# Seven quarter products in place of eight: one level of Strassen's algorithm in the second FFN product

## The chip, the cores and the metric

The kernel runs on one core of one Trainium2 chip. The metric is the device time of one execution in microseconds (us), as a median over runs. The span that the profile shows is 1.5 to 2 us shorter than that time, so I compare spans with spans and times with times. Ratios are the mean time of one kernel's fast runs over that of the other's fast runs of the same rounds, so they are not quite the ratios of the medians quoted beside them. Each comes with a 95% interval.

## The reference, cut to what matters

Eight batches. In each, 512 rows of x and 32 rows of a state attend to each other, in 8 heads of 64 columns; the result goes through an FFN with an exact GELU.

```python
scores = scale * x @ state^T;   a  = softmax(scores);   xread = a  @ state   # 512 rows a batch
scores2 = scale * state @ x^T;  a2 = softmax(scores2);  sread = a2 @ x       #  32 rows a batch
X = concat([xread, sread])                   # (8 x 544) rows of 512
h = X @ w_in                                 # 512 -> 2048
g = 0.5 * h * (1 + erf(h / sqrt(2)))
out = g @ w_out                              # 2048 -> 512: the "second FFN product"
```

For the 512 rows the kernel folds the state into the first weight (P = state @ w_in, per head), so the first product is only `a^T @ P`. The second product is the largest piece of work: for each batch a 512 x 2048 by 2048 x 512 matrix product.

## The kernel before

All operands are bf16, all sums are kept in f32 in PSUM. One batch goes through eight steps; in each step TensorE makes two blocks of 128 columns of h (`M`) and two quarters of an output tile (`U`), so that ScalarE's GELUs of one block run beside the matmuls of another. `[...]` marks cuts.

```python
def mm1(b, m):                               # first product, block m of 16
    [...]
    hp = ps_f.tile([128, S], FP32, name="hp", tag="f")
    for t in range(2):
        nc.tensor.matmul(hp, lhsT=Ps[b][:, t, m * 128:(m + 1) * 128],
                         rhs=atts[b].AT[:, :, t, :], start=(t == 0), stop=(t == 1))
    nc.scalar.activation(out=gs[b][:, m, :], in_=hp, func=AF.Gelu)

def mm2(b, q, j):                            # second product: 4 of the 16 blocks, rows j of 4
    [...]
    for m in range(4 * q, 4 * q + 4):
        nc.tensor.matmul(ps, lhsT=gs[b][:, m, j * 128:(j + 1) * 128],
                         rhs=w_out_bf[:, m, :], start=(m == 0), stop=(m == MC - 1))
    if q == 3:
        [...]
        evac(ps, [...])                      # VectorE copies PSUM to SBUF, SyncE issues the output

u = 17
for b in range(1, B):
    nb = b + 1
    for p in range(2 if b == 1 else 0, 8):
        k = 16 * b + 2 * p
        if p == (4 if b == 1 else 1) and nb < B:
            scores(nb, 0); scores(nb, 1)     # reads xT of the next batch
            [...]
        if b > 1 and p in (3, 4) and nb < B:
            norm(nb, p - 3)
        if p == (7 if b == 1 else 5) and nb < B:
            atr_dma(nb)                      # DMA transpose of the attention matrix: AT
        if p == 5 and nb + 1 < B:
            begin(nb + 1)
            rearr(nb + 1)                    # GpSimd copies of x
            xtr_dma(nb + 1)                  # DMA transpose of x: xT, two batches ahead
            rearr_ones(nb + 1)               # GpSimd copies of x
        M(k, k + 1)
        [...]
        while u < k - 4:
            U(u)
            u += 1
        if p == 2 and b > 1:
            burst([(b, 2), (b, 3)] + ([(nb, 0), (nb, 1)] if nb < B else []), b)   # P chunks
        if p == 6 and b + 3 < B:
            [...]
            load_x(b + 3)                    # GpSimd issues the load of x, three batches ahead
```

Both transposes and all outputs are issued by SyncE, into one DMA queue; the loads of x are issued by GpSimd into another.

The softmax here doesn't subtract the row's maximum and nothing guards it: scores larger than these inputs give would overflow.

Of the kernel before, what the change touches and what calls it, by code (L numbers as in the profile page):

```python
# [17 lines left out]
def kernel(  # L18
# [8 lines left out]
    nc = tc.nc  # L27
# [11 lines left out]
    persist = ctx.enter_context(tc.tile_pool(name="persist", bufs=1))  # L39
    xin = ctx.enter_context(tc.tile_pool(name="xin", bufs=3))  # L40
    att = ctx.enter_context(tc.tile_pool(name="att", bufs=2))
    gpool = ctx.enter_context(tc.tile_pool(name="gpool", bufs=3))
    opool = ctx.enter_context(tc.tile_pool(name="opool", bufs=4))
    PSUM = bass.MemoryType.PSUM
    ps_f = ctx.enter_context(tc.tile_pool(name="ps_f", bufs=4, space=PSUM))
    ps_o = ctx.enter_context(tc.tile_pool(name="ps_o", bufs=4, space=PSUM))

    ctx.enter_context(tc.manual_schedule())



# [5 lines left out]
    g_sr = persist.tile([128, MC, B * NS], BF16, name="g_sr")  # L57
    st_f = persist.tile([128, 2, D], FP32, name="st_f")
    st_bf = persist.tile([128, B, 2, D], BF16, name="st_bf")
    x0f = persist.tile([128, 4, 2, SJ * D], FP32, name="x0f")  # L60
    x0b = persist.tile([128, 4, SJ, 2, D], BF16, name="x0b")
    xT0 = persist.tile([128, 4, SJ, 128], BF16, name="xT0")
    sb0 = persist.tile([128, 2, 2, 2, NS], BF16, name="sb0")
    gate = persist.tile([128, HC], FP32, name="gate")
    hold = persist.tile([128, 1], BF16, name="hold")
# [61 lines left out]


    def keep_warm(n):
        ps = ps_o.tile([128, 512], FP32, name="warm_ps", tag="op")  # L130
        for _ in range(n):
            nc.tensor.matmul(ps[:, 0:128], lhsT=warm, rhs=warm, start=True, stop=True)

# [129 lines left out]

    def scores0(q):
        A = atts[0]
        pc = ps_o.tile([128, SJ, 2 * NS], FP32, name="pc", tag="op")
        for j in range(SJ):
            nc.tensor.matmul(  # L268
                pc[:, j, :],
                lhsT=xT0[:, q, j, :],  # L270
                rhs=sb0[:, q // 2, q % 2, :, :].rearrange("p u n -> p (u n)"),
                start=True,
                stop=True,
            )
        nc.scalar.activation(out=part0(A.e, q), in_=pc, func=AF.Exp, scale=scale)
# [76 lines left out]

    def sread(b):
        A = atts[b]
        pool, tag = (ps_o, "op") if b == B - 1 else (ps_f, "f")
        A.sr = pool.tile([128, 2, 65], FP32, name="sr", tag=tag)
        for t in range(2):
            for j in range(SJ):
                for c in range(HC):
                    nc.tensor.matmul(  # L360
                        A.sr[32 * c:32 * c + 32, t, :],
                        lhsT=A.e[:, 2 * j + t, 32 * c:32 * c + 32],
                        rhs=A.xo[:, j, c, 1 + 65 * t:66 + 65 * t],
                        start=(j == 0),
                        stop=(j == SJ - 1),
                    )
# [21 lines left out]

    Ps = {}

    def p_mm(b, f, pool, tag):
        if b not in Ps:
            Ps[b] = att.tile([128, 2, d_ff], BF16, name="P", tag="P")
        ps = [pool.tile([128, 512], FP32, name="p_ps", tag=tag) for t in range(2)]
        for c in range(HC):
            for t in range(2):
                nc.tensor.matmul(  # L397
# [11 lines left out]
        nc.vector.tensor_copy(out=dst[:, 1, :], in_=ps[1])  # L409

    def pmat(b, f):
        p_copy(b, f, p_mm(b, f, ps_f, "f"))



# [1 line left out]
    def burst(chunks, b_read=None):  # L417
# [2 lines left out]
        if first:  # L420
            sread(b_read)
        for i, (b, f) in enumerate(chunks):
            pool, tag = (ps_f, "f") if i < 2 else (ps_o, "op")
            done.append((b, f, p_mm(b, f, pool, tag)))
        for x in done[:2]:
            p_copy(*x)
        if b_read is not None and not first:
# [9 lines left out]
    def pmat00(h):  # L437
        if h == 0:
            Ps[0] = att.tile([128, 2, d_ff], BF16, name="P", tag="P")
        ps = [ps_o.tile([128, 256], FP32, name="p_ps", tag="op") for t in range(2)]  # L440
        for c in range(HC):
            for t in range(2):
                nc.tensor.matmul(
# [35 lines left out]
        return out[b * SB:b * SB + S, :].rearrange("(p j) n -> j p n", j=SJ)[j]  # L479


    def mm2_last(b, j):
        osb = opool.tile([128, d_model], FP32, name="osb", tag="osb")
        rows = out_rows(b, j)
        for n0, n1, pool, tag in ((0, 384, ps_o, "op"), (384, d_model, ps_f, "f")):
            ps = pool.tile([128, n1 - n0], FP32, name="opl", tag=tag)
            for m in range(MC):
                nc.tensor.matmul(  # L488
                    ps,
                    lhsT=gs[b][:, m, j * 128:(j + 1) * 128],  # L490
                    rhs=w_out_bf[:, m, n0:n1],
                    start=(m == 0),
                    stop=(m == MC - 1),
                )
            if n0 == 0:
                nc.vector.tensor_copy(out=osb[:, n0:n1], in_=ps)
                nc.sync.dma_start(out=rows[:, n0:n1], in_=osb[:, n0:n1])
            else:
                nc.scalar.copy(out=osb[:, n0:n1], in_=ps)  # L499
                nc.scalar.dma_start(out=rows[:, n0:n1], in_=osb[:, n0:n1])  # L500


    def mm2(b, q, j):
        if b == B - 1 and j == SJ - 1:
            return
        if q == 0:
            ops[b, j] = ps_o.tile([128, d_model], FP32, name="op", tag="op")
        ps = ops[b, j]
        for m in range(4 * q, 4 * q + 4):
            nc.tensor.matmul(  # L510
# [11 lines left out]
    def mm1_sr(m):  # L522
# [8 lines left out]
            )  # L531
        nc.scalar.activation(out=g_sr[:, m, :], in_=hp, func=AF.Gelu)

    def mm2_sr(s):
        ps = ps_f.tile([128, d_model], FP32, name="ops", tag="f")
        for m in range(MC):
# [14 lines left out]
    def mm2_m(b, m):  # L551
        for j in range(SJ):
            if m == 0:
                ops[b, j] = ps_o.tile([128, d_model], FP32, name="op", tag="op")
            nc.tensor.matmul(  # L555
                ops[b, j],
                lhsT=gs[b][:, m, j * 128:(j + 1) * 128],
                rhs=w_out_bf[:, m, :],
                start=(m == 0),
                stop=(m == MC - 1),  # L560
            )


    def M(*ms):
# [111 lines left out]


    u = 17
    for b in range(1, B):
        nb = b + 1  # L680
        for p in range(2 if b == 1 else 0, 8):
            k = 16 * b + 2 * p
            if p == (4 if b == 1 else 1) and nb < B:
                scores(nb, 0)
                scores(nb, 1)
                if b == 1:
                    norm(nb, 0)
                    norm(nb, 1)
            if b > 1 and p in (3, 4) and nb < B:
                norm(nb, p - 3)  # L690
            if p == (7 if b == 1 else 5) and nb < B:
                atr_dma(nb)
            if p == 5 and nb + 1 < B:
                begin(nb + 1)
                rearr(nb + 1)
                xtr_dma(nb + 1)
                rearr_ones(nb + 1)
            M(k, k + 1)
            if nb == B and p >= 4:
                for m in range(4 * p - 16, 4 * p - 12):  # L700
                    mm1_sr(m)
            while u < k - 4:
                U(u)
                u += 1
            if p == 2 and b > 1:
                burst([(b, 2), (b, 3)] + ([(nb, 0), (nb, 1)] if nb < B else []), b)
            if p == 6 and b + 3 < B:


                nc.gpsimd.tensor_copy(out=hold, in_=gs[b][:, 12, 0:1])  # L710
                load_x(b + 3)
            if p == 3 and b > 1:
                srt(b)
    while u < 16 * B - 4:
        U(u)
        u += 1
    mm2_sr(0)
    mm2_sr(1)
    U(*range(16 * B - 4, 16 * B - 1))
    mm2_last(B - 1, SJ - 1)  # L720


# [28 lines left out]
```

## Time and profile before

| | before |
|---|---|
| time, us | 216.77 median of 3 (216.36 to 216.99) |
| span in the profile, us | 215.3 |
| TensorE busy | 97% |
| VectorE, ScalarE, GpSimd busy | 38%, 57%, 21% |
| one steady batch in the chain, us | 22.90, without a gap |
| its second product, us | 8 x 1.73 = 13.84 |

The profile lists for each engine the time in which it was busy. The prediction below shows its lines and reads them.

### The profile page before, as it was taken

The page shows a single profiled execution, that of the slowest core. Times are in us where ns is not written, and L with a number is a line of the kernel's source. Part 1 is how long each engine was busy: PE and PEld are TensorE (multiplying, and loading weights), DVE is VectorE, ACT ScalarE, POOL GpSimd, SP SyncE. Part 2 cuts the span into 40 slices and gives each one's busy share as a digit, 9 for nine tenths or more (in the row PEclk, how much of TensorE's full clock was granted, in tenths as well). Part 3 has the DMA queues.
Part 4 walks back from the last instruction along what each step waited for, and adds up shares of the span by engine and source line. Part 5 has one row for each costly group of instructions (what it writes and reads, how often), then busy time and mean ns, then how long its engine had stood idle before and what let it go on. Part 6 is the DMA issues. An engine that isn't in the chain of part 4 may idle for free.

```text
span 215.3 us, 4019 instructions
## 1 busy us (share of the span) xinstructions
PE 208.1 (97%) x1667; PEld 102.4 (48%) x1667; DVE 80.8 (38%) x169; ACT 122.9 (57%) x220; POOL 45.7 (21%) x59
## 2 busy tenths in 40 slices
PE   7699999999999999999999999999999999999994
PEld 6445344444444445444544444444444444766443
DVE  2934474724039202850177005900392025000151
ACT  3954765687686447844874477645864444764000
POOL 8954303911023013301221130300000000000000
PEclk9999999999999999999999999999999999999999
DMA  6999999782822591428450873270225013000034
GB/s 205 173 172 204 205 193 176 182 212 52 97 97 100 97 140 44 160 45 140 63 194 3 156 88 131 67 144 4 100 97 53 0 49 148 3 0 0 6 104 185
DMA packets 40131, 23.11 MB, mean 107 GB/s; under 512 B 22064, under 2 KB 36656, under 8 KB 40112
## 3 DMA queue, kind: packets, MB, share of 16 engines
q0 software_dynamic: 13936, 8.10, 28.0%
q1 hardware_dynamic: 25488, 14.36, 25.1%
q10 hardware_dynamic: 688, 0.39, 0.6%
q8 instruction: 13, 0.21, 0.4%
q14 instruction: 6, 0.05, 0.1%
HBM read 17.30 MB, written 8.91 MB: 122 GB/s over the span
## 4 chain that ended last, share of the span: by engine, by line
PE 89%; DMA 7%; ACT 1%; POOL 0%; issue 0%; SPq 0%; DVE 0%
PE op L510 47%; PE hp L461 24%; DMA w_out_bf<-in_moe_w_out_dram 6%; PE p_ps L397 4%; PE hps L525 3%; PE ops L537 3%; DMA x0f<-in_x_dram 2%; PE op L555 2%; PE opl L488 2%; PE pt L305 1%; PE sr L360 1%; PE xT_ps L233 1%; POOL a L292 0%; PE pc L268 0%; ACT P L451 0%; ACT x0b L219 0%
## 5 line engine op out<-in xcount | busy, mean ns | idle before, releaser
L510 PE MATMUL op<-w_out_bf,g 128*128 128x512 bf16 x464 | 110.1, 379 | 0.4 <-DMA w_out_bf<-in_moe_w_out_dram 0.4
L468 ACT ACTIVATE g<-hp 128x512 bf16<-128x512 f32 x124 | 66.6, 600 | 53.4 <-PE hp L461 53.3
L510 PEld LDWEIGHTS <-g 128*128 128x128 bf16 x464 | 45.2, 98 | 54.5 <-issue 1.6
L461 PE MATMUL hp<-AT,P 128*128 128x512 bf16 x248 | 63.5, 379 | 0.5 <-ACT P L408 0.5
L474 DVE COPY osb<-op 128x512 f32<-128x512 f32 x31 | 21.4, 691 | 85.1 <-PE op L510 85.0
L461 PEld LDWEIGHTS <-P 128*128 128x128 bf16 x248 | 22.9, 98 | 25.8 <-issue 1.0
L408 ACT CAST P<-p_ps 128x512 bf16<-128x512 f32 x31 | 16.3, 595 | 13.6 <-PE p_ps L397 13.6
L409 DVE CAST P<-p_ps 128x512 bf16<-128x512 f32 x31 | 19.9, 682 | 7.5 <-PE p_ps L397 7.4
L201 POOL COPY x<-xb 128x1024 bf16<-128x1024 bf16 x12 | 12.2, 1045 | 33.5 <-DMA xb<-in_x_dram 28.2
L211 POOL COPY xo<-xb 128x1024 bf16<-128x1024 bf16 x12 | 12.2, 1051 | 20.1 <-PE sr L360 20.1
L325 DVE TENSOR_REDUCE cs<-e 128x16 f32<-128x512 bf16 x14 | 9.5, 676 | 4.0 <-ACT e L312 4.0
L397 PE MATMUL p_ps<-w_in_bf,sbd 64*32 64x512 bf16 x248 | 10.3, 381 | 0.0
L312 ACT ACT_TABLE_LOAD x7 | 9.0, 1283 | 1.8 <-issue 1.3
L328 DVE TENSOR_TENSOR a<-e,ics 128x512 bf16<-128x512 bf16 x14 | 9.7, 692 | 0.5
L474 DVE COPY osb<-ops 128x512 f32<-128x512 f32 x2 | 1.4, 692 | 22.5 <-PE ops L537 22.5
L468 ACT ACT_TABLE_LOAD x7 | 9.0, 1283 | 0.1
L499 ACT COPY osb<-opl 128x128 f32<-128x128 f32 x1 | 0.3, 266 | 15.2 <-PE opl L488 15.2
L555 PE MATMUL op<-w_out_bf,g 128*128 128x512 bf16 x32 | 7.7, 380 | 0.0
L312 ACT ACTIVATE e<-pt 128x512 bf16<-128x512 f32 x14 | 7.6, 594 | 0.1
L525 PE MATMUL hps<-XSR,w_in_bf 128*128 128x256 bf16 x64 | 7.6, 272 | 0.0
L710 POOL COPY hold<-g 128x1 bf16<-128x1 bf16 x4 | 0.8, 192 | 29.7 <-ACT g L468 29.7
L537 PE MATMUL ops<-w_out_bf,g_sr 128*128 128x512 bf16 x32 | 7.1, 379 | 0.0
(76 smaller groups left out, 123.2 us busy)
## 6 DMA issues: line engine op xcount, KB each, us to landing
out_dram<-osb SPq DMA_DIRECT2D x25, 256.0 KB, 2.4
xb<-in_x_dram POOLq DMA_DIRECT2D x7, 512.0 KB, 7.3
w_out_bf<-in_moe_w_out_dram POOLq DMA_DIRECT2D x4, 512.0 KB, 13.0
w_in_bf<-in_moe_w_in_dram POOLq DMA_DIRECT2D x6, 256.0 KB, 12.4
out_dram<-osb SPq DMA_DIRECT2D x12, 128.0 KB, 2.0
x0f<-in_x_dram SPq DMA_DIRECT2D x3, 256.0 KB, 3.8
w_in_bf<-in_moe_w_in_dram POOLq DMA_DIRECT2D x4, 128.0 KB, 4.1
out_dram<-osb SPq DMA_DIRECT2D x8, 64.0 KB, 1.7
```

The lines of the kernel that those rows point to most:

```text
L201: nc.gpsimd.tensor_copy(out=A.x4[:, :, :, 64 * t:64 * t + 64].rearrange("p j c d -> p c j d"), in_=src[:, t],)
L211: eng.tensor_copy(out=A.xo[:, :, :, 2 + 64 * t:66 + 64 * t].rearrange("p j c d -> p c j d"), in_=src[:, t],)
L312: nc.scalar.activation(out=A.e[:, :, 64 * half:64 * half + 64], in_=pt.rearrange("p j t c n -> p (j t) (c n)"), func=AF.Exp, scale=scale,)
L397: nc.tensor.matmul(ps[t][32 * c:32 * c + 32, :], lhsT=sbd[64 * t:64 * t + 64, b, c, 32 * t:32 * t + 32], rhs=w_in_bf[64 * t:64 * t + 64, c ...
L408: nc.scalar.copy(out=dst[:, 0, :], in_=ps[0])
L409: nc.vector.tensor_copy(out=dst[:, 1, :], in_=ps[1])
L461: nc.tensor.matmul(hp, lhsT=Ps[b][:, t, m * 128:(m + 1) * 128], rhs=atts[b].AT[:, :, t, :], start=(t == 0), stop=(t == 1),)
L468: nc.scalar.activation(out=gs[b][:, m, :], in_=hp, func=AF.Gelu)
L474: nc.vector.tensor_copy(out=osb, in_=ps)
L510: nc.tensor.matmul(ps, lhsT=gs[b][:, m, j * 128:(j + 1) * 128], rhs=w_out_bf[:, m, :], start=(m == 0), stop=(m == MC - 1),)
L525: nc.tensor.matmul(hp, lhsT=w_in_bf[:, c, m * 128:(m + 1) * 128], rhs=XSR[:, c, :], start=(c == 0), stop=(c == HC - 1),)
L537: nc.tensor.matmul(ps, lhsT=g_sr[:, m, s * 128:(s + 1) * 128], rhs=w_out_bf[:, m, :], start=(m == 0), stop=(m == MC - 1),)
```

## The change

The second product of batches 2 to 7 is cut into 2 x 2 quarters: tokens in two halves of 256, the 2048 hidden columns in two halves, the 512 output columns in two halves of 256. Strassen's scheme makes the four quarters of the output from seven quarter products in place of eight. With A for the quarters of g and B for those of w_out (the first index is the row half):

```
X3 = A00 (B01-B11)     X4 = A11 (B10-B00)         X6 = (A10-A00)(B00+B01)
X5 = (A00+A01) B11     X2 = (A10+A11) B00         X1 = (A00+A11)(B00+B11)     X7 = (A01-A11)(B10+B11)
C01 = X3+X5     C10 = X4+X2     C00 = X1+X4-X5+X7     C11 = X1-X2+X3+X6
```

The sums of weights are made once, by VectorE, into SBUF that held start-up data. The five sums of g quarters are made for each batch by VectorE. X5, X2 and X7 add onto the PSUM banks of X3, X4 and X1, and the rest of the combinations goes through small f32 tiles on VectorE (`s34`, `q`, the two output adds) and GpSimd (`u`, `v`). X3 and X6 of batch b run in its own steps 6 and 7, the other five in steps 0 to 4 of the next batch. The core of the diff, with cuts marked, some calls drawn together on one line, and the guards for the last batches left out. (The diff also cuts the pool of g from three buffers to two.)

```diff
-    opool = ctx.enter_context(tc.tile_pool(name="opool", bufs=4))
+    opool = ctx.enter_context(tc.tile_pool(name="opool", bufs=3))
 [...]
+    def g_sum(b, name):
+        [...]
+        t = apool.tile([128, MH, 256], BF16, name="gsum", tag="gsum")
+        nc.vector.tensor_tensor(out=t, in0=g_q(b, h0, k0), in1=g_q(b, h1, k1), op=op)
+    def x_mm(ps, lhs, rhs, first):
+        for j in range(2):
+            for m in range(MH):
+                nc.tensor.matmul(ps[:, j, :], lhsT=lhs[:, m, 128 * j:128 * j + 128], rhs=rhs[:, m, :], [...])
+    def X(b, name):
+        bank = {"3": 0, "4": 1, "5": 0, "2": 1, "1": 2, "6": 3, "7": 2}[name]
+        [...]
+        elif name == "4":
+            nc.vector.tensor_tensor(out=xs[b, "s34"], in0=ps, in1=xs[b, "s3"], op=ALU.add)
+        elif name == "5":
+            nc.scalar.copy(out=o, in_=ps)
+            nc.gpsimd.tensor_tensor(out=xs[b, "u"], in0=xs[b, "s34"], in1=o, op=ALU.subtract)
+        elif name == "1":
+            nc.vector.tensor_tensor(out=xs[b, "q"], in0=ps, in1=xs[b, "s34"], op=ALU.add)
+            nc.gpsimd.tensor_tensor(out=xs[b, "v"], in0=xs[b, "q"], in1=[...], op=ALU.subtract)
+        elif name == "7":
+            nc.vector.tensor_tensor(out=[...], in0=xs[b, 3], in1=xs[b, "v"], op=ALU.add)
+            x_out(b, 1)                      # 512 KB to HBM, issued by SyncE
+            nc.vector.tensor_tensor(out=[...], in0=ps, in1=xs[b, "u"], op=ALU.add)
+            x_out(b, 0)                      # 512 KB
 [...]
+    for b in range(2, B):
         for p in range(8):
+            if p == 5:
+                atr_dma(nb); begin(nb + 1); rearr(nb + 1); xtr_dma(nb + 1); rearr_ones(nb + 1)
             M(k, k + 1)
+            elif p < 5:
+                X(b - 1, "45217"[p])
+                for name in ("52", "1", "7", "", "")[p]:
+                    g_sum(b - 1, name)
+            if p == 5:
+                g_sum(b, "6")
+                p_run(nb, (0, 1), ((0, 3), (1, 2)))
+            if p == 6:
+                X(b, "3")
+            if p == 7:
+                p_run(nb, (2, 3), ((1, 2), None))
+                X(b, "6")
+            if p == 6 and b + 3 < B:
+                load_x(b + 3)
 [...]
+    X(b, "4") [...] mm2_sr(0); X(b, "5"); X(b, "2"); X(b, "1"); X(b, "7"); mm2_sr_last(1)
```

## The prediction

> **What bounds the kernel now.** I read the page's busy shares first, then the rows of clock and PE in slices, the chain that ended last, and the cost groups.
>
> ```profile
> PE 208.1 (97%) x1667; PEld 102.4 (48%) x1667; DVE 80.8 (38%) x169; ACT 122.9 (57%) x220; POOL 45.7 (21%) x59
> ...
> PE   7699999999999999999999999999999999999994
> ...
> PEclk9999999999999999999999999999999999999999
> ...
> PE 89%; DMA 7%; ACT 1%; POOL 0%; issue 0%; SPq 0%; DVE 0%
> ...
> L510 PE MATMUL op<-w_out_bf,g 128*128 128x512 bf16 x464 | 110.1, 379 | 0.4 <-DMA w_out_bf<-in_moe_w_out_dram 0.4
> ```
>
> TensorE is 97% busy at the full clock; 89% of the chain is matmuls, and the second FFN product (L510) is half the span. So only TensorE work counts, and any wait put into its queue is paid in full. The busy figure alone would not prove this, so I read one steady batch in the chain in order of time, and the busy time in that stretch:
>
> ```profile
> 104.84 0.47 PE pt L305 x16
> 105.31 0.86 PE hp L461 x4
> 106.17 1.73 PE op L510 x8
> ...
> 110.49 1.19 PE p_ps L397 x32
> 111.67 0.36 PE sr L360 x32
> 112.03 0.97 PE hp L461 x4
> ...
> 191.59 1.75 PE hps L525 x16
> ```
>
> ```profile
> 104.84:127.74 22.90, 22.90 (x183) 10.61 (x180) 8.73 (x17) 14.20 (x25) 5.31 (x7) 1.00 0.50 104
> ```
>
> The reader is to see that a batch takes 22.90 us and its pieces follow each other with no gap. VectorE (8.73) and ScalarE (14.20) have room on average. From the pieces: a 512-column matmul costs 1.73/8 = 216 ns, a 256-column one (L525 has them) 1.75/16 = 109 ns, four first-product matmuls 0.86 us, after a P burst 0.97.
>
> [...] Weight loads (98 ns each in the rows) are hidden behind 256 columns. So seven quarter products lose nothing to short matmuls. [...] No row of before has two dense bf16 inputs; I take 1.22 us for a sum of g quarters (8x256 elements). [...] the same normalisation took 1.57 us beside a GpSimd twin, 0.69 elsewhere.
>
> ```profile
> 9.31 1.11 POOL L292 TENSOR_TENSOR a<-e,ics 128x512 bf16<-128x512 bf16 x1
> ...
> 9.41 1.57 DVE L292 TENSOR_TENSOR a<-e,ics 128x512 bf16<-128x512 bf16 x1
> ```
>
> **The change part by part.**
>
> Gain. One batch's second product is 64 x 216 ns = 13.8 us; by Strassen 7 x 16 = 112 matmuls x 109 ns = 12.2 us. Saved 1.6 us a batch, 9.5 us for six. All of it is on the path. The burst of batch 7 before its GELUs also goes, and with it a ScalarE wait of 0.6 us in the chain near 179.5. Together -10.1.
>
> P chunks. The burst of four chunks (1.19) becomes two runs of two (0.56 each in the chain), each followed by the slower restart (0.97 against 0.86): about 0.15 a batch over five batches, and two single chunks in batch 1 (0.45 each, partly in place of others). +1.2.
>
> VectorE work a batch: five sums x 1.22 = 6.1 us, and four 0.69 us PSUM reads in place of four of the same. 8.7 + 6.1 is under 22, so it is not the bound. But it works in order, and here the path suffers:
>
> (a) X5 needs sum 5. It is queued behind the add of X4's result, which waits for X4's last matmul. From the end of X4's stream: about 0.19 of pipeline and semaphore (matmul rows of 379 ns at 216 spacing), add 0.69, sum 1.22, hand-overs and weight load 0.18 = 2.28 us. Meanwhile TensorE has scores 0.47 and first product 0.86 = 1.33. Stall 0.95 in four batches, 1.42 in the last (no scores): +5.2. GELUs and exponentials fit.
>
> (b) The fifth step's second P chunk takes the bank that X7 filled, which VectorE reads last. On VectorE stand after X1's read: a 0.22 copy, the second half of normalisation (0.68 + 0.25 + 0.69, gaps), the two output adds of 0.69. Counted from X7's end the second add ends at 1.55; TensorE wants the bank at 0.86 + 0.28 = 1.14. Stall 0.44 x 4: +1.8. The quarter product X7 itself finds its bank read just in time.
>
> (c) In batches 3 to 5 the rearranging GpSimd copies (1.04 each) now stand behind the new GpSimd subtraction v (1.1 like L292), and so begin just as that normalisation's two-input multiply does. If one copy blocks it, both adds slip 1 us: up to +2.9, I count 2.0.
>
> (d) Batch 1. The out-tile pool goes from four buffers to three. Batch 0's four evictions come together, and their transfers wait for a transpose on the same queue:
>
> ```profile
> 40.10 2.48 SPq L476 DMA_DIRECT2D out_dram<-osb  x4
> ```
>
> ```profile
> 41.23 0.69 DVE L474 COPY osb<-op 128x512 f32<-128x512 f32 x1 [1.03 <-PE op L510]
> ```
>
> ```profile
> DMA to landing us min/median/max: 3.3/3.5/3.8
> ```
>
> The first lands at 40.1 + 3.5 = 43.6, so the fourth eviction moves from 41.2 to 43.6 and the P copies behind it likewise; the first product that takes a P bank starts at 45.1 instead of 43.4: +1.7. Then steps of 1.73 us hold too little TensorE work for ScalarE's exponentials with two table loads of 1.28 us (that step is 5 us of ScalarE): I get another 1.2. Together +2.9. The five sums of weights (6.1 us of VectorE) lie there too but fit.
>
> (e) Transpose of the attention matrix. It queues after two 512 KB output transfers (1 MB in 3.2 us at the 330 GB/s that the four 256 KB ones show in their busiest microsecond), with 2.5 us of transfer of its own. I get a landing 7.5 us after X7 where the next batch wants it at 7.8; with an x load beside it in batches 3 and 4 about 0.5 late: +1.0.
>
> (f) Tail. X7 follows X1 directly and adds onto its bank, so it waits 0.85 for VectorE's read; eight small last transfers instead of two: +0.35. +1.2.
>
> Sum: -10.1 + 1.2 + 5.2 + 1.8 + 2.0 + 2.9 + 1.0 + 1.2 = +5.2, that is 222. The terms are worst-case in places (a stall that delays everything also gives later terms time), so I discount to +3.2: 220.0 us.
>
> **The rivals.** R1, the matmul count rules: the sums and adds hide in idle VectorE and only the gain stays, less P and tail: 216.8 - 10.1 + 2.4 = 209. For it: VectorE is 38% busy, the copy of weights is hidden, the schedule sits half a batch behind. Against it: the queue order of (a), which no average can cure. R2, VectorE latency takes TensorE's place at X5 and the banks: 219 to 222, my choice. R3, VectorE [...] becomes the bound: [...] (a) grows by 1.1 us five times, sum 7 comes after X7 wants it, and the time goes to 228 or more. For it: no row shows the fast form in tensor_tensor; against it: [...] a dense bf16 copy of 512 from PSUM takes 0.42 us where f32 takes 0.69. R4, transfers decide: an attention transpose that lands 2 us late in four batches adds 7 us to R1, 216; the transposes already took 3.1 to 4.3 us when alone.
>
> **Range and chances.** With all of (b) to (e) at half and (a) and (f) full: 216.8 - 10.1 + 1.2 + 5.2 + 3.8 + 1.2 = 218. With everything full and (c) at 2.9: 223. I widen this to 215 to 225. Faster by over 2% needs under 212.4: the losses would have to be under 5.7 us, while (a) alone is 5.2: chance 0.10. Slower needs over 221.1, where the undiscounted sum lies: 0.40. The rest 0.50.
>
> **What would show it.** Right: 672 matmuls of 128x256 in the quarter products at 109 ns spacing; a wait of TensorE before X5 on the g sum, 0.9 to 1.5 us, once in each of batches 3 to 7; the g sums at 1.2 us; a wait before the second P chunk for an output add; the fourth eviction of batch 0 waiting for a transfer; steady batches of 22.5 to 24 us. Wrong: no TensorE gaps at X5 (R1), g sums of 2.3 us (R3), or first products that wait for AT (R4). If X5 does not wait, the time will be near 210 and (a) was my error.

Some of this goes beyond the rows of before. The 1.22 us of a sum of g was taken, not read; after shows it (1.22 as the median of thirty, 1.21 to 2.25). The 2.3 us of R3 is a supposition; the longest sum in after is those 2.25. And that a GpSimd copy holds up the multiply under (c) is the author's estimate from one pair: the 1.57 us above is the only multiply of before that ran beside GpSimd, and the fourteen others that are alike in shape (0.69 us each) ran beside none.

## More of the kernel before

The columns are output and input, issuing queue, kind and count, and the median in us.

```profile
xT<-x SPq DMA_TRANSPOSE x6, 4.4
AT<-a SPq DMA_TRANSPOSE x6, 3.3
```

## The result, and the profile after

The changed kernel is correct and slower:

| | before | after |
|---|---|---|
| time, us | 216.56 median of 4 (215.86 to 216.99) | 227.46 median of 4 (224.73 to 227.62) |
| ratio | | 1.047, 95% 1.041 to 1.053 |
| span, us | 215.3 | 225.8 |
| TensorE busy, us | 208.1 | 205.1 |
| VectorE busy | 38% | 56% |
| granted clock of the runs | 0.998 to 1.0 (its runs beside the experiments) | 0.977 to 0.986 |

Their clock is below 1 and their times spread by 2.9 us. We will see that the kernel itself brings this about. The prediction was 220.0, with 215 to 225 as its range; the measured median lies 7.5 us above the one and 2.5 us above the other.

First the page: busy shares, the rows of TensorE and of its clock in 40 slices, and the shares of the chain that ended last.

```profile
PE 205.1 (91%) x1955; PEld 129.6 (57%) x1955; DVE 126.3 (56%) x204; ACT 132.2 (59%) x238; POOL 66.5 (29%) x71
...
PE   7788999978999889997699989998999899999990
...
PEclk9999999999999999999799999999999999999997
...
PE 60%; DMA 18%; POOL 9%; DVE 5%; ACT 3%; issue 2%; DVEq 0%; POOLq 0%; ACTq 0%
```

TensorE does less work, as planned, but no longer without gaps, and matmuls make only 60% of the chain where they made 89%. Transfers have come in with 18%. The 20th slice, at 107 to 113 us, has both the emptiest TensorE (but for the end) and a clock of 0.7. Which waits these are, the view of TensorE's waits tells (who waited for what: us in total, how often, longest; start-up waits left out):

```profile
PE pt L319 <- DMA xT<-x: 4.9, 3, 3.5
PE xp L621 <- DVE gsum L615: 1.8, 2, 1.1
PE hp L473 <- DVE P L422: 1.8, 1, 1.8
...
PE xp L621 <- DVE q L665: 0.8, 1, 0.8
PE p_ps L410 <- DVE osb L486: 0.7, 1, 0.7
```

The largest is one that the prediction does not have: the scores of the next batch (L319) wait for xT, the transpose of x. Then come predicted ones: the sum of g for X5, the P chunk of batch 1, and X7's wait for `q`. The last is a bank in batch 2, held by an eviction of batch 1; it is not the bank that the prediction had under (b).

The worst place, in the chain in order of time (start, us, what):

```profile
99.89 9.46 DMA xT<-x
...
109.39 0.64 PE pt L319 x16
...
111.33 2.98 PE xp L621 x16
...
115.64 1.75 PE xp L621 x16
```

The transpose was issued at 99.89 and landed 9.46 us later. The same sixteen matmuls of a quarter product then take 2.98 us the first time and 1.75 us the second. The windows around it say why (from and to, length, us, busy time of PE, PEld, DVE, ACT and POOL with counts, granted clock, DMA share, GB/s):

```profile
105.70:109.30 3.60, 0.14 (x2) 0.00 (x0) 3.35 (x4) 0.52 (x1) 0.00 (x0) 1.00 0.67 89
109.30:110.30 1.00, 0.91 (x19) 0.68 (x20) 0.74 (x1) 0.47 (x1) 0.00 (x0) 1.00 0.00 0
110.30:113.70 3.40, 3.40 (x16) 2.10 (x15) 0.00 (x0) 2.99 (x5) 0.00 (x0) 0.50 0.00 0
```

TensorE idles for 3.6 us, and 1 us later its clock is 0.50 for 3.41 us (110.31 to 113.72). That is half of 3.41 or 1.7 us lost again. How much idle time it takes is taken up in the experiments.

Why did xT land so late? SyncE's queue and GpSimd, from the timeline (start, us, engine, line, operation):

```profile
96.25 0.89 SPq L635 DMA_DIRECT2D out_dram<-oh  x2
97.23 2.56 SPq L362 DMA_TRANSPOSE AT<-a  x1
99.89 3.50 SPq L268 DMA_TRANSPOSE xT<-x  x1
```

```profile
93.77 1.26 POOL L667 TENSOR_TENSOR v<-q,oh 128x512 f32<-128x512 f32 x1 [3.36 <-DVE XSR L400]
94.98 2.48 POOL L215 COPY x<-xb 128x1024 bf16<-128x1024 bf16 x2
97.41 3.02 POOL L225 COPY xo<-xb 128x1024 bf16<-128x1024 bf16 x2
...
100.49 0.91 POOL L117 DMA_DIRECT2D xb<-in_x_dram  x1
```

Two things meet here. The queue of SyncE has 1 MB of outputs at 96.25, then AT, then xT; before, the five outputs of a batch were issued from 84.78 to 89.04, 5 us ahead of AT at 94.41. And the load of x starts at 100.49, 0.6 us after xT, where before it started 3.0 us after it (98.72 and 95.74). A third thing did not count in this batch: the copies that xT reads (L215) stand behind the new subtraction `v` on GpSimd, but they end at 97.5, and SyncE is busy with the issue of AT until 99.8. So the landing times became these, where before had medians of 7.3 for the load, 3.3 for AT and 4.4 for xT:

```profile
xb<-in_x_dram POOLq DMA_DIRECT2D x1, 512.0 KB, 9.0
AT<-a SPq DMA_TRANSPOSE x1, 5.7
xT<-x SPq DMA_TRANSPOSE x1, 9.5
```

In the four batches that transpose x at this place xT landed 7.7, 9.5, 7.2 and 4.7 us after its issue. The first three made TensorE wait; the fourth, without a load beside it, did not. In the worst of them xT was issued 5.8 us before TensorE wanted it (99.89 and 105.68), where before it was 9.1 us (95.74 and 104.84). So 3.3 us went by the later issue and 5.1 by the longer way to landing, and 3.7 remained as a wait.

By the start times of successive matmuls, after loses 12.1 us in its larger gaps between 40 and 220 us: 5.4 for xT (0.89 at 83.0, 3.71 at 105.6, 0.75 at 132.9), 2.1 for the sum before X5 (0.82 at 156.7, 1.29 at 178.7), 2.8 in batch 1 (1.93 at 44.3, 0.62 and 0.28 at 53.5), 0.85 at 72.9 for a bank, and 0.95 at 213.9 before X7. (The view of waits counts a little less for each, since it begins when the last matmul has ended.)

### The profile page after: what moved, and what is told of

It reads as the page before. It is cut to its first block, busy times and chain, and to the rows that moved or that the text cites. A ratio compares the mean times of both kernels' runs of the same rounds, so it can differ in the third digit from the quotient of the medians.

```text
span 225.8 us, 4658 instructions
## 1 busy us (share of the span) xinstructions
PE 205.1 (91%) x1955; PEld 129.6 (57%) x1955; DVE 126.3 (56%) x204; ACT 132.2 (59%) x238; POOL 66.5 (29%) x71
## 4 chain that ended last, share of the span: by engine, by line
PE 60%; DMA 18%; POOL 9%; DVE 5%; ACT 3%; issue 2%; DVEq 0%; POOLq 0%; ACTq 0%
PE xp L621 25%; PE hp L473 16%; DMA xT<-x 11%; PE op L499 7%; DMA w_out_bf<-in_moe_w_out_dram 6%; PE hps L514 3%; POOL x L215 2%; PE p_ps L410 2%; POOL w_in_bf L105 2%; PE op L568 2%; DMA out_dram<-osb 2%; PE opl L532 2%; PE ops L550 2%; DVE osb L486 1%; POOL xo L225 1%
## 5 line engine op out<-in xcount | busy, mean ns | idle before, releaser
L621 PEld LDWEIGHTS <-gsum 128*128 128x128 bf16 x480 | 47.0, 99 | 16.2 <-issue 3.6
L615 DVE TENSOR_TENSOR gsum<-g 128x2048 bf16<-128x2048 bf16 x30 | 40.5, 1381 | 7.9 <-ACT g L480 6.8
L621 PE MATMUL xp<-ws,gsum 128*128 128x256 bf16 x288 | 34.4, 273 | 0.8 <-DVE q L665 0.8
L660 POOL TENSOR_TENSOR u<-s,oh 128x512 f32<-128x512 f32 x6 | 9.5, 1576 | 81.3 <-ACT oh L658 81.3
L621 PE MATMUL xp<-w_out_bf,gsum 128*128 128x256 bf16 x192 | 24.1, 282 | 1.8 <-DVE gsum L615 1.8
L499 PE MATMUL op<-w_out_bf,g 128*128 128x512 bf16 x96 | 23.7, 379 | 0.4 <-DMA w_out_bf<-in_moe_w_out_dram 0.4
L621 PE MATMUL xp<-ws,g 128*128 128x256 bf16 x192 | 22.9, 273 | 0.0
L621 PEld LDWEIGHTS <-g 128*128 128x128 bf16 x192 | 18.8, 98 | 4.3
L215 POOL COPY x<-xb 128x1024 bf16<-128x1024 bf16 x12 | 13.5, 1154 | 16.5 <-DMA xb<-in_x_dram 11.6
L499 PEld LDWEIGHTS <-g 128*128 128x128 bf16 x96 | 9.1, 97 | 12.0 <-issue 1.6
L655 DVE TENSOR_TENSOR s<-xp,s 128x512 f32<-128x512 f32 x6 | 4.2, 692 | 20.5 <-PE xp L621 20.5
L667 POOL TENSOR_TENSOR v<-q,oh 128x512 f32<-128x512 f32 x6 | 7.6, 1267 | 22.3 <-DVE XSR L400 20.3
```

What stands on the lines that cost most here:

```text
L215: nc.gpsimd.tensor_copy(out=A.x4[:, :, :, 64 * t:64 * t + 64].rearrange("p j c d -> p c j d"), in_=src[:, t],)
L615: nc.vector.tensor_tensor(out=t, in0=g_q(b, h0, k0), in1=g_q(b, h1, k1), op=op)
L621: nc.tensor.matmul(ps[:, j, :], lhsT=lhs[:, m, 128 * j:128 * j + 128], rhs=rhs[:, m, :], start=(first and j == 0 and m == 0), stop=(m == M ...
```

## The experiments

The theory after the trace (T): the arithmetic saving is real, but it is eaten by three separate waits, xT (with a clock drop behind it), the sum before X5, and the fourth output buffer in batch 1; undo all three and the time falls to about 217 (10.3 us less, as the expectation of e4_all3 has it). The rivals: (R-gain) the seven products do not save what the count says, so that no repair can go below before; (R-vector) VectorE, with its waits for GpSimd, is too full, and each repair only moves the wait; (R-clock) the low clock is given from outside and has nothing to do with the kernel's gaps.

All results first; "clock" is the mean granted clock of each run. Before had medians of 216.4 to 216.9 in the same rounds. The label slow goes to a run more than 1.5% above the fastest run of the same kernel. In kernels with gaps this label may have cut off runs that only had more clock drops.

| kernel | time, us: median (range) | ratio to before, 95% | clock of runs |
|---|---|---|---|
| after | 227.46 (224.73 to 227.62) | 1.047 (1.041 to 1.053) | .977 to .986 |
| e1_early_xt | 222.16 (220.66 to 224.04, one labelled slow) | 1.023 (1.017 to 1.028) | .989 to .997 |
| e2_sum5_first | 225.01 (221.23 to 227.67, two labelled slow) | 1.025 (1.020 to 1.030) | .980 to .996 |
| e3_out4 | 223.84 (221.32 to 224.44) | 1.030 (1.024 to 1.037) | .978 to .998 |
| e4_all3 | 214.81 (214.08 to 215.33) | 0.991 (0.988 to 0.993) | .992 to .998 |
| e5_load_early | 227.74 (225.19 to 228.00) | 1.046 (1.039 to 1.054) | .971 to .986 |
| e6_filled | 224.83 (224.34 to 225.14) | 1.035 (1.030 to 1.040) | .992 to .997 |
| e7_uv_dve | 223.13 (222.90 to 223.49) | 1.028 (1.023 to 1.033) | .994 to .998 |
| e8_tuned | 214.32 (213.00 to 216.35, one labelled slow) | 0.984 (0.976 to 0.992) | .992 to .995 |
| e9_tail_load | 216.46 (215.92 to 217.59) | 1.000 (0.997 to 1.002) | .988 to 1.0 |
| e10_eight (wrong result) | 225.37 (224.81 to 226.62) | 1.039 (1.036 to 1.041) | .993 to .999 |
| e11_tail | 211.55 (210.66 to 214.84, one labelled slow) | 0.976 (0.972 to 0.980) | .992 to 1.0 |

### One repair at a time, and all three

**Transpose x earlier.** The copies that it reads and the transpose itself move from step 5 to step 2, where no output stands in front.

```diff
+            if p == 2 and nb + 1 < B:
+                begin(nb + 1)
+                rearr(nb + 1)
+                xtr_dma(nb + 1)
             if p == 5:
                 if nb < B:
                     atr_dma(nb)
                 if nb + 1 < B:
-                    begin(nb + 1)
-                    rearr(nb + 1)
-                    xtr_dma(nb + 1)
                     rearr_ones(nb + 1)
```

> Only the rearranging and the transpose of the batch after next are moved from step 5 to step 2 of each Strassen batch, ahead of the output transfers and of the other transpose. Theory A (late transposes in the shared queue are the largest cost: TensorE waited 0.7, 3.5 and 0.6 us for xT, and the half clock of 3.4 us behind the longest wait cost 1.7 us more): no wait for xT, clock 1.00, and 4 to 5 us less than the changed kernel (about 223), not the full 6.5, because the wait of X5 for its sum, hidden behind the late scores in three batches, comes back with 0.7 to 0.9 us each. Theory B (the clock is lowered by the denser matmuls themselves): the waits go, but the clock stays at 0.98. Theory C (the transposes are slow by themselves beside the loads): xT still lands too late, time within 1 us of the changed kernel's 227.5.

Measured: 222.16 us, 5.3 under after. No matmul waits for xT any more; one in the steady part landed 4.5 us after its issue. In its place the sum before X5 now stops TensorE in five batches in place of two:

```profile
PE xp L621 <- DVE gsum L615: 3.8, 5, 1.1
PE hp L473 <- DVE P L422: 2.2, 1, 2.2
```

By the start times it is 0.82 in four batches and 1.29 in the last, 4.6 us together. In after the late xT had hidden the wait in three of them, because the sum was done by the time that the scores could begin. This is why waits read from one trace cannot be added up: one covers another.

**Sum 5 ahead of X4's add.** The same instruction is issued earlier in VectorE's queue, so that it no longer stands behind the add of X4's result.

```diff
             elif p < 5:
+                if p == 0:
+                    g_sum(b - 1, "5")
                 X(b - 1, "45217"[p])
-                for name in ("52", "1", "7", "", "")[p]:
+                for name in ("2", "1", "7", "", "")[p]:
```

> Only the sum of g quarters for X5 is put ahead of the add that reads X4. Theory A (X5's wait is pure queue order on VectorE): the wait of about 0.7 to 1.1 us in the last two batches goes, in the three batches with a late xT nothing can be won, 1.5 to 2 us less than the changed kernel (225.5 to 226). Rival (VectorE is full, so the wait only moves to X2 or X1): the time stays at 227.5 and a new wait for a g sum shows.

Measured: X5 waits no more; the view of waits has no line for it. The xT gap stays:

```profile
PE pt L319 <- DMA xT<-x: 3.4, 2, 3.3
```

The time is the least clear: 221.23, 223.15, 226.88 and 227.67, with clocks of .996, .990, .982 and .980 in the same order. The slow runs are those with the low clock; the ratio of 1.025 rests on the two runs that are labelled fast, and the median of all four, 225.0, is only 2.5 us under after.

**Four output buffers, as before.**

```diff
-    opool = ctx.enter_context(tc.tile_pool(name="opool", bufs=3))
+    opool = ctx.enter_context(tc.tile_pool(name="opool", bufs=4))
```

> Only the output tiles get their fourth buffer back. If the fourth eviction of batch 0 is what holds the P copies and with them the first product near 44 us (1.8 us in the trace), 1.5 to 2 us less than the changed kernel (about 225.7). If the steps behind it are bound by ScalarE's exponentials and table loads anyway, which then take up the gain, 0 to 0.5 us less.

Measured: 223.84 us, 3.6 under after, and the gap at 44 us with its wait for P is gone from the trace. The largest wait for xT stays (3.72 us), with a half-clock stretch right behind it. A gain of 3.6 is more than the 1.5 to 2 expected; the gap was 1.93, the start-up of this profile is 1.1 us shorter (its first `sr` matmul runs at 20.5, that of after at 21.6), and one run has a clock of .998, so without any such stretch but at the end. I have not taken the rest apart. In after this gap came as predicted: the fourth eviction waited for the first output to land, and VectorE's copy of P stood behind it, as its lines say (the bracket holds the idle time before it and what ended that):

```profile
45.11 0.69 DVE L486 COPY osb<-op 128x512 f32<-128x512 f32 x1 [3.60 <-DMA out_dram<-osb]
...
46.45 0.59 PE L473 MATMUL hp<-AT,P 128*128 128x512 bf16 x2 [1.77 <-DVE P L422]
```

**All three** (the edits above together).

> All three edits together. Theory A: the sum of the three and of the X5 waits that the first edit uncovers: 6.5 + 2 + 1.8 off 227.5, about 217, within 1 us of the kernel before, clock 1.00. If one cause stands for all (the late transposes shift everything behind them), the three do not add up and the time is 221 to 223.

Measured: 214.81 us, 12.65 under after and 0.991 of before, with a spread of 1.25 us. By their medians the three repairs alone give 5.3, 2.5 and 3.6 us, which sum to 11.4. The 214.81 is 2 us better than the 217 expected. R-gain falls: with the waits out of the way the kernel is faster than before, by 0.9% (0.7 to 1.2). The page's busy line and the window of one steady batch:

```profile
PE 202.2 (95%) x1955; PEld 129.6 (61%) x1955; DVE 125.0 (59%) x204; ACT 131.7 (62%) x238; POOL 66.2 (31%) x71
```

```profile
101.83:123.54 21.71, 21.71 (x232) 15.01 (x228) 15.32 (x22) 15.54 (x28) 9.09 (x8) 1.00 0.53 110
```

A steady batch takes 21.71 us, all of them busy on TensorE, where it took 22.90. The difference of 1.19 comes out of the chain: the seven quarter products take 12.37 in place of 13.84 (-1.47); the two runs of P chunks take 0.80 and 0.56 where one burst took 1.19 (+0.17); and one more first product follows a P run at 0.97 in place of 0.86 (+0.11).

### What is a quarter product worth?

In the kernel with all three repairs X2's sixteen matmuls run twice. The result is wrong (relative error 0.60), its type and shape are right.

```diff
         x_mm(ps, lhs, rhs, first)
+        if name == "2":
+            x_mm(ps, lhs, rhs, False)
```

> The version with three edits (214.8 us), with one quarter product of each batch run twice into its bank (the result is wrong on purpose): eight quarter products instead of seven, as many columns as the plain product has. If TensorE's queue is the bound there and a quarter product is worth its 16 x 109 ns = 1.75 us, as the gain of the prediction assumes, 6 x 1.75 = 10.5 us more, about 225.3. If VectorE or the transfers set the pace of the batches, so that a product fewer is worth little, 4 us more or less.

Measured: 225.37 us, 10.56 over the same kernel without it. Six batches of 1.75 us are 10.5. TensorE's busy time grows from 202.2 to:

```profile
PE 213.4 (95%) x2051; PEld 139.1 (62%) x2051; DVE 124.4 (55%) x204; ACT 131.7 (59%) x238; POOL 66.1 (29%) x71
```

So with the waits removed TensorE is the bound, and the product that Strassen saves is worth its whole length.

### Is it the load beside the transpose?

From after, the load of x moves from step 6 to step 2, away from the transpose; the order of the transposes stays.

```diff
-            if p == 6 and b + 3 < B:
-                nc.gpsimd.tensor_copy(out=hold, in_=gs[b][:, 12, 0:1])
+            if p == 2 and b + 3 < B:
+                nc.gpsimd.tensor_copy(out=hold, in_=gs[b][:, 4, 0:1])
                 load_x(b + 3)
```

> Changed kernel with one move: the load of x three batches ahead starts in step 2 instead of step 6, so it no longer runs beside the two transposes; their place in the queue is left. Theory L (the load beside them makes xT late; without one, in batch 5, xT landed in 4.7 us instead of 7.2 to 9.5): xT lands in 4.5 to 6 us, the waits for it fall from 5.3 us in sum to under 1, no half clock near 106, 222 to 224 us. Theory Q (the place in the queue behind 1 MB of output and the other transpose makes it late): xT still lands in 7 us or more, the 3.7 us wait stays, 226 to 227.5.

Measured: xT lands after 4.4, 5.7, 6.0 and 4.7 us in place of 7.7, 9.5, 7.2 and 4.7, and no matmul waits for it. The second and third of these:

```profile
xT<-x SPq DMA_TRANSPOSE x1, 5.7
xT<-x SPq DMA_TRANSPOSE x1, 6.0
```

So the load beside it was what made xT late enough to be waited for. Yet the time is 227.74, no better than after. Two things took the place of the xT wait. The sum before X5, no longer hidden, costs 4.6 us in five batches by the start times. And in batch 2 a new gap of 3 us opened: the load's move shifted the rearranging copies onto a normalisation multiply, which took 2.81 us beside them, and the eviction behind it on VectorE, which TensorE needed, came late:

```profile
68.70 2.02 POOL L215 COPY x<-xb 128x1024 bf16<-128x1024 bf16 x2
...
70.41 2.81 DVE L342 TENSOR_TENSOR a<-e,ics 128x512 bf16<-128x512 bf16 x1
70.66 2.00 POOL L225 COPY xo<-xb 128x1024 bf16<-128x1024 bf16 x2
```

```profile
PE p_ps L410 <- DVE osb L486: 2.8, 1, 2.8
```

The multiply of the batch's other half takes 0.69 us (at 75.47), those of batches 3 to 6 in after 0.69 to 0.92, and this one 2.81; it ends 0.56 us after the last of the copies, so that the rest of one copy and two whole ones went by in its time. Half-clock stretches followed the gap at 43 us and the one at 73.6; the mean clock of this profile is 0.971.

### Does the idle time bring the low clock?

From after: dummy matmuls of 512 columns with zero weights fill the two large gaps, eight in batch 1 and fifteen ahead of the scores that wait for xT. They write into the PSUM tile that the next real matmul overwrites.

```diff
+        for _ in range(fill):
+            nc.tensor.matmul(hp, lhsT=warm, rhs=w_out_bf[:, 0, :], start=True, stop=True)
 [...]
-        M(16 + 2 * p, 17 + 2 * p)
+        mm1(1, 2 * p, 8 if p == 2 else 0)
+        mm1(1, 2 * p + 1)
 [...]
-                scores(nb, 0)
+                scores(nb, 0, 15 if b == 4 else 0)
```

> Changed kernel with dummy matmuls (zero weights, overwritten results) put into its two longest waits of TensorE: eight of 512 columns (1.7 us) near 44 us and fifteen (3.2 us) near 106 us. The waits stay as long, so as work it saves nothing. If idle TensorE is what takes the clock to half for 3.41 us (two such stretches in the runs at a mean clock of 0.977, one at 0.986), the clock stays at 1.00 up to the end in every run, and the time falls by 1.7 us a stretch to 224 to 226, with little spread. If the clock falls by itself or with the load, it is still at 0.977 to 0.986 and the time at 227.5 or a little over.

(That the runs at 0.977 have two stretches is an estimate: the profile of after, at 0.986, has one before its end, and 1.7 us of 225.8 take 0.008 off the mean.)

Measured: 224.83 us, 2.6 under after, though TensorE has more to do. The spread falls from 2.9 to 0.8 us, and the clocks are .992 to .997. The clock row has no dip but at the end, where TensorE has finished:

```profile
PEclk9999999999999999999999999999999999999997
```

R-clock falls: the lower clock of after, and most of its spread, come from TensorE's own gaps. How long must a gap be? The length alone does not tell. In the profiled runs, after the start-up, gaps of 3.71 (after), 3.72 (four buffers), 2.40 (the transpose moved early), 2.19 and 2.98 (the load moved early) were followed by a half-clock stretch, and gaps of 3.42 and 2.44 (sum 5 first), 2.09 (e8_tuned) and 1.93 (after) were not. The windows tell. Within one profile the starts of these stretches lie whole multiples of 3.413 us apart (33 of them, 112.64 us, in after; 11, 9 and 43 in the load experiment). Cut each profile into windows on that grid, and in these profiles a stretch follows a window in which TensorE was idle for 2.02 us or more. These are the window before the stretch in after, in the early transpose and in the early load (columns as above; idle is the length less the first busy time), and last the most idle one that no stretch followed, in sum 5 first:

```profile
106.90:110.31 3.41, 0.92 (x19) 0.69 (x20) 3.14 (x3) 0.48 (x1) 0.00 (x0) 1.00 0.21 26
43.14:46.55 3.41, 1.17 (x6) 0.42 (x5) 1.98 (x4) 0.94 (x3) 1.63 (x2) 1.00 0.72 220
42.45:45.86 3.41, 1.39 (x6) 0.53 (x6) 1.75 (x3) 1.36 (x3) 1.81 (x2) 1.00 0.70 216
105.10:108.51 3.41, 1.43 (x21) 0.96 (x22) 1.72 (x2) 0.98 (x2) 0.00 (x0) 1.00 0.14 18
```

The gap of 3.42 us in the last one (103.66 to 107.08) lies across a border of the grid, and no window got more than 1.98 of it. So in these 13 profiles, after their first 20 us, the border lies between 1.98 and 2.02 us of idle time in one window, and a gap above 2 us brought the stretch or not, as it fell on the grid (2.19 and 2.40 did, 2.44 and 3.42 did not). (The ends of matmuls are modelled, so 2.0 is not exact, and no run was made to test it.)

### Is GpSimd's share of the work the trouble?

From the kernel with all three repairs, `u` and `v` move from GpSimd to VectorE: in after the three sums of g that ran beside `u` took 2.23 to 2.25 us, where the median of all thirty is 1.22.

```diff
-            nc.gpsimd.tensor_tensor(out=xs[b, "u"], in0=xs[b, "s34"], in1=o, op=ALU.subtract)
+            nc.vector.tensor_tensor(out=xs[b, "u"], in0=xs[b, "s34"], in1=o, op=ALU.subtract)
```

(and `v` alike)

> The version with three edits (214.8 us), with the two subtractions on GpSimd moved to VectorE[...] (VectorE gets 1.4 us more a batch). If contention of GpSimd with the two-input instructions of VectorE is on the path (step (c) of the prediction, 2.0 us), 1 to 2 us less than 214.8. If the longer sums of g (1.4 us in the mean, 2.25 at most, against 1.22 for the sums of weights) are off the path, within 0.7 us of 214.8.

Measured: 223.13 us, 8.3 over the kernel that it came from, so a miss of both expectations, with no clock drop before the end. X7 now waits for `q` in five batches, where it had waited once, in the tail:

```profile
PE xp L621 <- DVE q L665: 3.8, 5, 0.9
```

With two more subtractions on VectorE, the sums behind them come late for X1 (0.45 us in each of two batches, by the start times) and `q` comes late for X7. So R-vector is half right: VectorE is not full (15.3 of the 21.7 us of a steady batch), but its order has so little slack that two instructions put into it at the wrong place stop TensorE in four batches and the tail. Leaving `u` and `v` to GpSimd, as the change did, is right here.

### How far does it go?

From the kernel with all three repairs: batch 1's pieces in another order, batch 2's normalisation behind its evictions, one P bank from the other pool, and a tail that ends on X7 with its outputs in smaller pieces.

```diff
-            if p in (3, 4) and nb < B:
+            if p in (3, 4) and nb < B and b > 2:
 [...]
-                    p_run(nb, (0, 1), ((0, 3), (1, 2)))
+                    p_run(nb, (0, 1), ((0, 3), (1, None)))
 [...]
     X(b, "1")
+    mm2_sr(0)
+    mm2_sr(1)
     X(b, "7")
-    mm2_sr_last(1)
```

> The version with three edits, and the waits that it still shows taken away: 0.9 us near 50 (a second product moved to the step with the exponentials), 0.85 near 70 (evictions ahead of the normalisation), 0.23 in four batches (the second P chunk in another bank), 0.95 in the tail and the 5.5 us from TensorE's end to the last landing (the products of the state rows between X1 and X7, fewer and smaller last transfers). If these lie on the path one after the other: 214.8 - 0.9 - 0.85 - 0.9 - 0.95 - 2.2, about 209, 3.5% faster than the kernel before. If other waits take their place, 211 to 214.

Measured: 214.32 us, 0.984 of before, against 0.991. Most of the gain was given back to a new wait, for AT (2.2 us in two batches, 1.9 the longest), whose transpose landed 7.6 us after issue beside a load. The kernel also still ended 6 us after TensorE.

The next version lets the outputs of the last batch leave as soon as each is made, and moves two loads of x to step 3, to free AT's transpose.

```diff
         elif name == "5":
 [...]
+            if b == B - 1:
+                nc.sync.dma_start(out=rows[:, 0:2, NH:], in_=o)
 [...]
+            if p == (6 if b == 2 else 3) and b + 3 < B:
+                [...]
+                load_x(b + 3)
```

> The tuned version with two more moves. The last batch's outputs leave as soon as they exist (its trace ends 6.0 us after TensorE, the kernel before 2.9), and the loads of batches 3 and 4 start in step 3, so that they no longer run beside the transpose that TensorE waited for (2.1 and 0.45 us). If both lie on the path: 214.3 - 2.9 - 2.5, about 209. If a wait of the state's or of the attention transposes takes their place, 211 to 213.

Measured: 216.46 us, equal to before, so a miss. The tail did get shorter, 4.0 us after TensorE's end. But in batches 3 and 4, whose loads moved, a P bank came 1.5 us late, in batch 3 behind a normalisation multiply that took 2.95 us. Nor did AT's wait go away:

```profile
89.29 2.95 DVE L342 TENSOR_TENSOR a<-e,ics 128x512 bf16<-128x512 bf16 x1
89.67 2.02 POOL L225 COPY xo<-xb 128x1024 bf16<-128x1024 bf16 x2
```

```profile
PE p_ps L410 <- DVE oh L638: 3.0, 2, 1.5
PE hp L473 <- DMA AT<-a: 1.9, 2, 1.3
```

The last version keeps the short tail and puts the loads back.

```diff
-            if p == (6 if b == 2 else 3) and b + 3 < B:
+            if p == 6 and b + 3 < B:
                 nc.gpsimd.tensor_copy(out=hold, in_=gs[b][:, 12, 0:1])
                 load_x(b + 3)
```

> The tuned version (214.3 us) with only the tail of the last trial, the loads back in step 6: in that trial the span ended 4.0 us after TensorE instead of 6.0, and what it lost came from v waiting behind the load on GpSimd. If so, 2.0 us less than 214.3, 212 to 212.6, with the wait for the attention transpose (2 us) still there; if the early loads had nothing to do with the loss, about 216.5 again.

Measured: 211.55 us over six runs, 0.976 of before (0.972 to 0.980), correct, and the fastest kernel. It is faster than before; whether by 2% stays unclear, as that bound lies just inside the interval. The long multiply is gone:

```profile
90.11 0.92 DVE L342 TENSOR_TENSOR a<-e,ics 128x512 bf16<-128x512 bf16 x1
90.42 2.49 POOL L225 COPY xo<-xb 128x1024 bf16<-128x1024 bf16 x2
```

So the early load brought it about. But not as in the load experiment: here the copies come 0.31 us after the start of the multiply, there 0.38, so they were not pushed onto it. Nor had `v` waited for the load: it began 0.20 us after `q` ended there and 0.14 here. Here the multiply ended before the copies (91.03 and 92.91), there after them (92.24 and 91.69); why is not shown. AT's wait, expected to stay at 2 us, is 0.6, because its transpose landed after 5.9 us in place of the 7.6 of e8_tuned with the load at the same place; I cannot say why, so not all of the gain is this edit's. TensorE is busy for 96%:

```profile
PE 201.2 (96%) x1939; PEld 128.1 (61%) x1939; DVE 124.6 (59%) x205; ACT 131.2 (62%) x237; POOL 66.1 (31%) x71
```

## Why the prediction was wrong

The prediction had the saving and most of the waits. It named 220 and the undiscounted sum 222; the kernel took 227.5. By its own steps:

| step | predicted, us | measured, us |
|---|---|---|
| gain of six batches, and the wait of 0.6 | -10.1 | about -9.4 (6 x 1.47 in the repaired kernel, and 0.6) |
| P chunks | +1.2 | +0.28 a batch with (b) in it |
| (a) sum before X5 | +5.2 | +2.1 in after; +4.6 where xT is in time |
| (b) bank of the second P chunk | +1.8 | 0.23 x 4 (in the +0.28); another bank, in batch 2, +0.85 once |
| (c) GpSimd beside the multiply | +2.0 | no wait of TensorE in after; up to 3 us in other orders |
| (d) batch 1 | +2.9 | +2.8 (1.93, 0.62, 0.28) |
| (e) transposes | +1.0 | AT +0.23 once; **xT +5.4, and +1.7 by the clock** |
| (f) X7 and tail | +1.2 | +0.95 and +2.5 |
| start-up, in no step | 0 | +1.3 in the profiled run |
| sum; discounted to | +5.2; +3.2 | +10.5 (spans) |

- **The gain was right**, a little large: each quarter product takes 1.75 us, not 16 x 109 ns = 1.74, and two of the seven in a steady batch take 1.77 and 1.85. The eighth product, put back, cost 10.56 us.
- **Step (e) is the one that failed.** It asked whether AT, queued behind 1 MB of outputs, would land in time, and found a narrow yes with 1.0 us for two batches. That part was right almost to the digit: in batch 3 AT landed 7.4 us after X7's end, where TensorE wanted it at 7.5 (predicted 7.5 and 7.8), and in batch 4 it was 0.23 us late. But the step passed over the transpose of x, which follows AT in the same queue and has the x load beside it. The prediction worked out the copies behind `v` under (c), and the load under (e), and never followed both to xT, the last in the queue. It cost 5.4 us of TensorE's time and, by the clock, 1.7 more. Rival R4 ("transfers decide") was the right kind of answer, for the wrong transpose.
- **The clock was no term at all.** The prediction read a full clock in the kernel before and took it over. In a kernel with gaps above 2 us this is not safe: the one half-clock stretch of the profiled run cost 1.7 us.
- **(a) was right in mechanism and nearly in size**: 0.82 where it said 0.95, 1.29 where it said 1.42. The sum that it counted with 1.22 us took 1.22 us there, and in the median of all thirty; the longest, 2.25, ran beside GpSimd's `u`. So R3's slow sum of 2.3 us, a supposition, falls. In after only two of its five instances could show, since a late xT covers the other three. That is one reason why moving the transpose alone gained 5.3 and not 7 us, and why moving the load alone gained nothing; the other is the gap in batch 1 with its clock drop in the one, and the multiply of 2.81 us in the other.
- **(c) was off.** In after the multiplies of batches 3 to 6 took 0.69 to 0.92 us, and TensorE did not wait. In other orders a multiply beside the copies took longer than I gave it (2.81 us in e5_load_early, 2.95 in e9_tail_load), but not wherever the copies fall on the multiply: in the fastest kernel they do, and it takes 0.92.
- **(b) and the P chunks were too high, in part by slips of the sum.** (b) has 1.55 less 1.14 as 0.44, but it is 0.41, and 0.23 was measured. Two P runs of 0.56 and one more slow restart of 0.11 for one burst of 1.19 make 0.04 a batch by the prediction's own figures, not 0.15; without the bank's wait the trace has 0.05.
- **(d) was right** in cause and size.
- **(f)**: X7's wait was 0.95 for a predicted 0.85. The tail was mis-sized. From the end of the last copy to the end of the span it took 5.1 us (225.8 less 220.69) in place of 2.6 (215.3 less 212.69), for a predicted +0.35; eight small transfers stand behind two outputs of 512 KB there. In e9_tail_load and e11_tail the outputs leave earlier, and it is 3.1. The chain's last pieces, before and then after:

```profile
208.89 3.51 PE opl L488 x32
...
212.42 0.27 ACT osb L499
```

```profile
216.89 3.51 PE opl L532 x32
...
220.42 0.27 ACT osb L542
```

The discount from 222 to 220 leaned on stalls that give later terms time. They did (a late xT hid (a) in three batches), but the missing term was larger than what that gave. That the kernel without the xT wait, e1_early_xt, took 222.2, the undiscounted sum, is partly luck: in after, (b), (c) and the P chunks had been put too high by 3.6 us, and the tail, the start-up and the bank in batch 2 took 4.4 that were not counted.

Does it close? The measured rows of the table, with 1.4 for P in five batches, sum to 9.8 of the 10.5 us. Between after and the kernel with the three repairs the spans differ by 12.2 us (225.8 and 213.6). The gaps that went are 1.93 + 5.35 + 2.1 = 9.4, the clock drop 1.7, and the tail gives back 0.4. Another 1.2 lies in the start-up, which none of the edits touches: the matmuls that read the second part of w_out began at 23.70 in the one, when it landed, and at 22.46 in the other, without a wait for it. That makes 11.9. Between the repaired kernel and before the spans differ by -1.7. Here I count -9.4 for the gain, 1.4 for P, 0.9 and 0.85 for what is left of batches 1 and 2, 0.95 for X7, and 2.9 for the tail (5.5 in place of 2.6), -2.4 together. The missing 0.7 I have not placed; batch 1's single P chunks, which the prediction put at part of 1.2, lie in it.

How much of xT's lateness belongs to its place in the queue and how much to the load? In the worst batch the later issue took 3.3 us of its time. Of the way to landing, 4.4 us before became 5.7 in the load experiment, which keeps the queue and takes the load away, and 9.5 with both: 1.3 for the queue and 3.8 for the load. In the next batch the load's part is only 1.2 (7.2 and 6.0). What stays open is why it differs so: these are single profiles.

## What to carry to other kernels

When a change moves transfers and the work in front of them, follow each queue to its last entry, not only to the one that you moved: here xT, the last, was issued later and ran beside a load, and landed after 9.5 us in the worst batch where before had a median of 4.4. Add a term for the clock as soon as a wait of more than about 2 us can arise on TensorE: here such a wait cost another 1.7 us (3.71 us in after), or nothing (3.42 in e2_sum5_first), as it fell on the grid of 3.413 us that these profiles show. And read waits as covering each other: repair the largest, look again, and expect the next to come out, up to its own full size.
